# A fused attention and two-MoE kernel on one core: another cost model for spreading attention units, and six places of PSUM for the first MoE once attention is over

## The chip, the cores and the metric

The kernel runs on one core of one Trainium2 chip. The metric is the device time of one execution in microseconds. Before the change the median of three runs is 749.09 us (747.17 to 750.77).

## What is computed

Attention over 4 batches, 8 heads, 576 tokens and 64 channels per head, with a mask by blocks of 64 tokens; its result, as x of 576 x 512 per batch, goes through a first MoE block and that through a second:

```
scores = scale * q @ k.T, masked by blocks of 64;  attn = softmax(scores);  x = attn @ v
xk = mu_k*x + (1-mu_k)*x_prev;  xr = mu_r*x + (1-mu_r)*x_prev        # x_prev: x shifted by a token
k = relu(xk @ w_k);  v = (k*k) @ w_v;  r = sigmoid(xr @ w_r);  x = r*v    # first MoE, 512 -> 1024 -> 512
h = gelu(x @ w_in);  u, v = halves of h;  v = layernorm(v)*g_ln
x = x + (u * (w_sg @ v + b_sg)) @ w_out                                # second MoE
```

All products are of full float32 precision: a factor is split into a high and a low float32r part, and three products stand for one.

## The kernel before

**Attention** is cut into 64 units, one for each batch, head and kind. A unit of kind LO holds tokens 0 to 319, one of kind HI tokens 320 to 575. Their order (L245) is batches 0 and 1 LO (units 0 to 15), batches 0 and 1 HI (16 to 31), then the same for batches 2 and 3 (32 to 63). A unit has three steps: `emit_S` (scores into the PSUM tiles SA and SB, maxima on VectorE, exponentials on ScalarE, normalisation of P on VectorE), `emit_T` (P is turned over through PSUM tile T on TensorE; ScalarE copies out the high part PH, VectorE the low part PL) and `emit_PV` (the product with V into PSUM tile O; ScalarE copies one half out as otmp, VectorE adds the other into xT). Scores run two units ahead of the other steps (`LAG`, L434). The first 16 units (`DIRECT`) use whole float32 products, which the planner's model prices twice as high as split ones.

**The first MoE** (`moe1`, L508) runs over eight halves of 288 tokens (L496), each with 8 tiles of wk, 4 of wr and 4 of wv. A tile is accumulated in PSUM over 12 products of 128x288 (24 for wv). Before a half, `mix` (L475) makes its xh and xl from xT in four chunks of two heads each, so a half needs the attention units of its batch. ScalarE empties a wk tile with a Relu into R (two buffers); the square, the copy kh and the low part kl follow on ScalarE and GpSimd.

**The order of work.** The program is written as a stream of small steps. `Order` holds a model of time in TensorE nanoseconds (`cost`, L112): `pe` moves it on, `at` puts an evacuation into it. While `moe1` runs, the loop at L666 asks at every tick how much of attention should have been issued by now. It emits pieces while `spent_a - base < target(x)` (L671), where x counts halves and `spent_a` is the model time of attention so far. `target` (L652) runs in straight lines between knots: at x = i - 0.15 the units that half i needs must be there (`need`, `MIX_AT`). Its height is `cum(n)`, a sum of `UNIT_NS`, 2000 ns for a LO unit and 3120 for a HI one. What is still missing when the knot is reached is emitted at once (L674). The tile framework then orders each engine's queue by a schedule of its own, so places are read below from the built order.

**PSUM** before the second MoE has eight banks: M with two buffers, T with two, O and SA with one each, and SB, two banks wide. `mtile1` (L148) gives the first MoE its tiles, always from M. When attention is over, T, O, SA and SB stand empty until the second MoE opens its own pool (L703).

**The tail.** With the last unit emitted (L677) the loads of w_in start, and each tick splits two pieces of w_in (`w_split`, L212): per piece Abs on ScalarE (L218), four passes over 128x512 on VectorE (L219, L220, L222, L224), a copy `w` on ScalarE (L227) and a last pass on VectorE (L229). Then x of batch 0 comes back from DRAM and is split into XHL (L661, L693). The second MoE begins with tiles V (`stage_v`, L746).

Of the kernel before, what the change touches and what calls it, by code (L numbers as in the profile page):

```python
# [17 lines left out]
B, H, S = 4, 8, 576  # L18
# [2 lines left out]
CH0 = [0, 64, 192, 320, 448]  # L21
CHN = [64, 128, 128, 128, 128]
CHE = [64, 192, 320, 448, 576]

F64_MIN = struct.unpack("f", struct.pack("I", 896 << 20))[0]
F64_MAX = struct.unpack("f", struct.pack("I", (1151 << 20) - 1))[0]
# [15 lines left out]
class Order:  # L42
# [12 lines left out]
    def pe(self, ns):  # L55
        self.run(self.t)
        self.t += ns
# [43 lines left out]


DIRECT = 16
XT_BUFS = 8
MIX_AT = 0.85
G = 2
X0_AT = 0.55
CONV2 = 2
UNIT_NS = [2000, 3120]


def cost(n):  # L112
    return n / 2.4 + 13
# [3 lines left out]
def fused_kernel(ctx: ExitStack, tc: tile.TileContext, first, qkv_lo, qkv_hi, mu,  # L117
# [21 lines left out]
    def ptile(tag, cols, bufs):  # L139
# [5 lines left out]
        r.append(key)  # L145
        return ps([128, cols], F32, tag, bufs), key

    def mtile1():  # L148
        t, key = ptile("M", 512, 2)
        return t[:, 0:HF], key  # L150

    def mm(out, lhsT, rhs, start=False, stop=False):
# [130 lines left out]
    def split_v(n):  # L283
# [8 lines left out]
        copy(nc.scalar, V[:, 0:nj, odd, :], v)  # L292
        sub(nc.gpsimd, V[:, 0:nj, 1 - odd, :], v, V[:, 0:nj, odd, :].bitcast(F32))

    def emit_S(n):
        b, h, kind = units[n]
        order.need(("sp", n))
        Q, K, KL = splits.pop(n)
        chunks = CHUNKS[kind]
        if n < H and n % 2 and kind == LO:  # L300
            (sa, ka), (sb, kb) = ptile("M", 512, 2), ptile("M", 512, 2)
        else:
            (sa, ka), (sb, kb) = ptile("SA", 512, 1), ptile("SB", 1024, 1)
        stc = {0: sa[:, 0:64], 1: sa[:, 64:256], 2: sb[:, 0:320], 3: sa[:, 0:448]}
        if kind == HI:
            stc[4] = sb[:, 224:800]
        skc = [ka, ka, kb, ka, kb]
        P = probs[n] = pbuf[n % 2]
        pieces = {c: [(0, 288), (288, 576)] if c == 4 else [(0, CHE[c])] for c in chunks}
        pe(sum((2 if n >= DIRECT else 4) * cost(e - a) for c in chunks for a, e in pieces[c])  # L310
           + cost(64) * (n >= DIRECT) * sum(c > 0 for c in chunks))
        mx, sm = smax[n % 4], ssum[n % 4]
        t0, t1 = TOKENS[kind]
        nb = atile([128, 5], F32, "nb", 4)
        rr = atile([128, 5], F32, "rr", 4)
        for c in chunks:
            q0, m, e, st = CH0[c] - TOKENS[kind][0], CHN[c], CHE[c], stc[c]
            for k0, k1 in pieces[c]:
                o = st[0:m, k0:k1]
                if n < DIRECT:  # L320
                    mm(o, Q[:, q0:q0 + m], K[:, k0:k1], start=True, stop=True)
                    continue
                mm(o, Q[:, q0:q0 + m], K[:, k0:k1], start=True)
                if c > 0 and k1 == e:
                    mm(st[:, e - 64:e], mask_l, mask_r)
                mm(o, Q[:, q0:q0 + m], KL[:, k0:k1], stop=True)

        def red(cs):
            for c in cs:
                m, e, st = CHN[c], CHE[c], stc[c]  # L330
                nc.vector.tensor_reduce(out=mx[0:m, c:c + 1], in_=st[0:m, 0:e], axis=AX.X, op=ALU.max)
            s = slice(cs[0], cs[-1] + 1)
            nc.scalar.activation(out=nb[:, s], in_=mx[:, s], func=AF.Copy, scale=-0.125)

        def exp(cs):
            for c in cs:
                m, e, st, po = CHN[c], CHE[c], stc[c], POFF[c]
                nc.scalar.activation(out=P[0:m, po:po + e], in_=st[0:m, 0:e], func=AF.Exp,  # L338
                                     scale=0.125, bias=nb[0:m, c:c + 1], accum_out=sm[0:m, c, 0:1])

        def norm():
            cs = slice(chunks[0], chunks[-1] + 1)
            nc.vector.tensor_reduce(out=rr[:, cs], in_=sm[:, cs], axis=AX.X, op=ALU.add)
            nc.vector.reciprocal(out=rr[:, cs], in_=rr[:, cs])
            for c in chunks:
                m, e, o = CHN[c], CHE[c], POFF[c]

                nc.vector.tensor_scalar(out=P[0:m, o:o + e], in0=P[0:m, o:o + e],  # L348
                                        scalar1=rr[0:m, c:c + 1], scalar2=None, op0=ALU.mult, op1=ALU.add,
                                        accum_out=junk[0:m, c:c + 1])  # L350

        parts = [[0, 1, 2]] if kind == LO else [[3], [4]]
        t = 0
        for cs in parts:
            w = sum(CHE[c] for c in cs)
            sk = [skc[c] for c in cs]
            at(t, lambda cs=cs: red(cs), *sk)
            t += 1.1 * w
            at(t + 100, lambda cs=cs: exp(cs), *sk, ("P", n))
        at(t + 1.2 * w + 500, norm, ("P", n))  # L360
# [32 lines left out]
    def emit_PV(n):  # L393
        b, h, kind = units[n]
        order.need(("sv", n))
        V = vs.pop(n)
        odd = h % 2
        ot, ok = ptile("O", 512, 1)
        order.need(("PT", n))
        prods = PRODS[kind]  # L400
        pe(sum((2 if n >= DIRECT else 4) * cost(p[4]) for p in prods))
        t0, t1 = TOKENS[kind]
        for x, (j, u, src, q0, nq) in enumerate(prods):
            for i, part in enumerate(trans[n, u]):
                v = V[:, 64 * j:64 * j + 128] if n < DIRECT else V[:, j].rearrange("p a d -> p (a d)")
                mm(ot[:, q0 - t0:q0 - t0 + nq], v,
                   part[:, src:src + nq], start=x == 0 and i == 0, stop=x == len(prods) - 1 and i == len(trans[n, u]) - 1)
        for u in range(len(GROUPS[kind])):
            trans.pop((n, u))
        if (b, h // 2) not in xt:  # L410
            t = xt[b, h // 2] = mtile([128, S + 2], F32, "xT", XT_BUFS)
            nc.gpsimd.memset(t[:, 0:1], 0.0)
        t = xt[b, h // 2]
        r0, r1 = 64 * odd, 64 - 64 * odd
        tmp = atile([128, 320], F32, "otmp", 1)
        w = t1 - t0

        def ev1():
            copy(nc.scalar, tmp[r0:r0 + 64, 0:w], ot[r1:r1 + 64, 0:w])

        def ev2():
            nc.vector.tensor_tensor(out=t[r0:r0 + 64, 1 + t0:1 + t1], in0=ot[r0:r0 + 64, 0:w],  # L422
                                    in1=tmp[r0:r0 + 64, 0:w], op=ALU.add)

        def ev():
            copy(nc.scalar, t[r0:r0 + 64, 1 + t0:1 + t1], ot[0:64, 0:w])

        if n < DIRECT:
            at(0, ev, ok, ("x", b, kind))
            return  # L430
        at(0, ev1, ok)
        at(600, ev2, ok, ("x", b, kind))
# [208 lines left out]
    for i in range(1, len(halves)):  # L641
        if need[i] > knots[-1][1]:
            knots.append((i - 1 + MIX_AT, need[i]))
    unit_t = [UNIT_NS[kind] for b, h, kind in units]
    base = spent_a

    def cum(n):
        return sum(unit_t[H:n])

    all_t = cum(NU)  # L650

    def target(x):  # L652
# [13 lines left out]
    for x in moe1():  # L666
# [10 lines left out]
        if done >= NU and phase2 is None:  # L677
# [2 lines left out]
            order.need(*[k for k in list(order.due) if k[0] in ("x", "ps", "PT", "P")])  # L680
            acm.__exit__(None, None, None)
            phase2 = True
            wcm, wtile = pool("moe2w", side="right")

            def wt2(shape, dt):
# [283 lines left out]
```

## Time and profile before

| what | value |
|---|---|
| median of three runs | 749.09 us |
| time of the profiled execution | 752.42 us |
| its span, first to last instruction | 750.5 us |
| mean granted TensorE clock | 0.973 of full speed |
| PE busy | 699.5 us (93%), 4824 matmuls |
| DVE / ACT / POOL busy | 529.5 / 434.8 / 329.4 us |

The profiled execution is 3.3 us longer than the median. Matmuls overlap in the pipeline, so a group's mean duration (some 300 ns) is not what one costs in a stream: that is read from a stretch of time and the number of matmuls in it. A wait is given in brackets in the rows, with what ended it.

### The profile page before, as it was taken

The numbers are of one execution on the slowest core, as the hardware profiler recorded it, in microseconds if no ns is written. First come the engines' busy times: TensorE is split into PE (matmuls) and PEld (weight loads), VectorE is DVE, ScalarE is ACT, GpSimd is POOL, SyncE is SP. The second block draws the span as 40 slices with busy tenths as digits, with TensorE's granted clock in tenths as the row PEclk, the third lists the DMA queues.
The fourth block names the chain that finished last, engine by engine and source line by source line (L and its number), as shares of the span: only waits on it lengthen the run. The fifth ranks groups of instructions, "written<-read, shape, count | busy, mean of one in ns | idle before, by whom it ended". The sixth has DMA issues, their size and how long they took to land.

```text
span 750.5 us, 13615 instructions
## 1 busy us (share of the span) xinstructions
PE 699.5 (93%) x4824; PEld 660.2 (88%) x4824; DVE 529.5 (71%) x1306; ACT 434.8 (58%) x1247; POOL 329.4 (44%) x381
## 2 busy tenths in 40 slices
PE   7878989998799899999899989988999999999998
PEld 5567869998799799999799979977999999999997
DVE  5999987778885766674885988479698736636323
ACT  4878768866795697794795788355361212122020
POOL 1437657834583386483584466134034204103021
PEclk9998999999999999999999999989999999999999
DMA  8571124223212222223222220062460120120101
GB/s 264 216 257 34 33 92 147 64 87 104 83 59 69 78 69 77 58 83 103 79 90 80 79 94 4 25 232 64 142 251 2 38 89 1 41 87 1 56 9 64
DMA packets 30724, 65.78 MB, mean 88 GB/s; under 512 B 5280, under 2 KB 16544, under 8 KB 30656
## 3 DMA queue, kind: packets, MB, share of 16 engines
q1 hardware_dynamic: 30512, 64.91, 26.5%
q8 instruction: 38, 0.62, 0.4%
q14 instruction: 30, 0.25, 0.1%
q10 hardware_dynamic: 144, 0.00, 0.0%
HBM read 55.47 MB, written 9.44 MB: 86 GB/s over the span
## 4 chain that ended last, share of the span: by engine, by line
PE 68%; DVE 14%; ACT 11%; DMA 3%; issue 3%; POOL 1%; SPq 0%; ACTq 0%; POOLq 0%; DVEq 0%
PE M L153 39%; PE O L153 14%; PE V L153 5%; PE T L370 5%; PE SB L153 3%; PE SA L153 3%; ACT P L338 2%; DVE u L222 2%; ACT PH L157 2%; DVE u L224 1%; DVE u L219 1%; DVE P L348 1%; DVE t L484 1%; DVE u L220 1%; DMA w<-w_k_dram 1%
## 5 line engine op out<-in xcount | busy, mean ns | idle before, releaser
L153 PE MATMUL M<-xh,w 128*128 128x288 f32 x768 | 178.8, 310 | 12.4 <-ACT xh L157 6.3
L153 PEld LDWEIGHTS M<-xh,w 128*128 128x128 f32 x768 | 133.0, 195 | 16.8 <-ACT R L535 7.9
L153 PE MATMUL M<-xl,w 128*128 128x288 f32 x384 | 117.2, 306 | 1.2 <-DVE xl L168 1.2
L153 PE MATMUL M<-kh,w 128*128 128x288 f32 x512 | 111.9, 300 | 3.7 <-ACT w L227 3.7
L168 DVE TENSOR_TENSOR PL<-T,PH 128x256 fp32r<-128x256 f32 (+3 forms) x128 | 68.9, 542 | 30.5 <-ACT PH L157 29.6
L153 PEld LDWEIGHTS M<-kh,w 128*128 128x128 f32 x512 | 84.7, 189 | 4.1 <-ACT w L227 4.1
L370 PE MATMUL T<-ident,P 128*128 128x128 f32 x480 | 83.5, 286 | 4.2 <-DVE P L348 2.4
L157 ACT ACTIVATE PH<-T 128x384 fp32r<-128x384 f32 (+4 forms) x144 | 68.0, 478 | 30.0 <-PE T L370 27.5
L168 POOL TENSOR_TENSOR KL<-qkv,K 128x576 fp32r<-128x576 f32 (+1 forms) x48 | 60.6, 1263 | 54.3 <-ACT K L157 40.8
L348 DVE TENSOR_SCALAR_CACHE_REDUCE P<-P,rr 64x64 f32<-64x64 f32 (+3 forms) x160 | 79.7, 536 | 1.1
L153 PEld LDWEIGHTS M<-xl,w 128*128 128x128 f32 x384 | 75.3, 196 | 2.2 <-DVE xl L168 1.8
L153 PE MATMUL M<-kl,w 128*128 128x288 f32 x256 | 76.0, 297 | 0.0
L847 POOL TENSOR_TENSOR gt<-gt,U 128x288 f32<-128x288 f32 x32 | 29.3, 920 | 100.5 <-DVE gt L843 100.4
L370 PEld LDWEIGHTS T<-ident,P 128*128 128x128 f32 x480 | 59.7, 147 | 9.1 <-issue 3.0
L168 POOL TENSOR_TENSOR xl<-t,xh 128x288 fp32r<-128x288 f32 x48 | 41.0, 855 | 49.3 <-ACT xh L157 46.8
L168 POOL TENSOR_TENSOR kl<-R,kh 128x288 fp32r<-128x288 f32 x64 | 57.8, 915 | 10.2 <-ACT kh L157 9.6
L168 POOL TENSOR_TENSOR w<-u,w 128x512 fp32r<-128x512 f32 x24 | 35.5, 1482 | 59.4 <-ACT w L227 59.4
L153 PE MATMUL O<-PH,V 128*128 128x256 f32 (+2 forms) x208 | 58.8, 294 | 3.0 <-DVE xT L422 3.0
L168 POOL TENSOR_TENSOR V<-qkv,V 128x320 fp32r<-128x320 f32 (+1 forms) x48 | 39.4, 820 | 45.2 <-ACT V L157 30.4
L153 PE MATMUL O<-PL,V 128*128 128x256 f32 (+2 forms) x208 | 56.3, 289 | 1.6 <-DVE PL L168 1.6
L153 PE MATMUL O<-gh,w 128*128 128x288 f32 x256 | 53.3, 294 | 0.0
L153 PE MATMUL M<-XHL,w 128*128 128x288 f32 x384 | 53.1, 295 | 0.0
(155 smaller groups left out, 1845.1 us busy)
## 6 DMA issues: line engine op xcount, KB each, us to landing
qkv<-qkv_hi_dram SPq DMA_DIRECT2D x32, 576.0 KB, 3.8
qkv<-qkv_lo_dram SPq DMA_DIRECT2D x16, 416.0 KB, 3.3
x2d<-x SPq DMA_DIRECT2D x32, 144.0 KB, 2.0
X<-x2d SPq DMA_DIRECT2D x4, 1152.0 KB
outT_dram<-o SPq DMA_DIRECT2D x32, 144.0 KB, 1.8
w<-w_k_dram SPq DMA_DIRECT2D x8, 512.0 KB
w<-w_v_dram SPq DMA_DIRECT2D x8, 512.0 KB, 7.6
w<-w_in_dram SPq DMA_DIRECT2D x8, 512.0 KB, 8.9
```

The lines of the kernel that those rows point to most:

```text
L153: nc.tensor.matmul(out=out, lhsT=lhsT, rhs=rhs, start=start, stop=stop)
L157: nc.scalar.activation(out=out, in_=in_, func=AF.Copy)
L168: eng.tensor_tensor(out=out, in0=a, in1=b, op=ALU.subtract)
L219: nc.vector.tensor_scalar(out=v, in0=v, scalar1=F64_MIN, scalar2=F64_MAX, op0=ALU.max, op1=ALU.min)
L220: nc.vector.tensor_scalar(out=u, in0=u, scalar1=3, scalar2=0x3FFFFFFF, op0=ALU.logical_shift_left, op1=ALU.bitwise_and)
L222: nc.vector.scalar_tensor_tensor(out=u, in0=high, scalar=-0x40000000, in1=u, op0=ALU.bitwise_and, op1=ALU.bitwise_or)
L224: nc.vector.scalar_tensor_tensor(out=u, in0=low, scalar=29, in1=u, op0=ALU.logical_shift_right, op1=ALU.bitwise_or)
L338: nc.scalar.activation(out=P[0:m, po:po + e], in_=st[0:m, 0:e], func=AF.Exp, scale=0.125, bias=nb[0:m, c:c + 1], accum_out=sm[0:m, c, 0:1])
L348: nc.vector.tensor_scalar(out=P[0:m, o:o + e], in0=P[0:m, o:o + e], scalar1=rr[0:m, c:c + 1], scalar2=None, op0=ALU.mult, op1=ALU.add, acc ...
L370: nc.tensor.transpose(t[:, o:o + 128], P[:, POFF[c] + CH0[j]:POFF[c] + CH0[j] + 128], ident)
L484: nc.vector.scalar_tensor_tensor(out=t1, in0=x[:, s0 + 1:s0 + 1 + HF], scalar=mu_t[:, i, c:c + 1], in1=t1, op0=ALU.mult, op1=ALU.add)
L847: nc.gpsimd.tensor_tensor(out=gt, in0=gt, in1=U[b][:, m, fs], op=ALU.mult)
```

## The change

Two things. First, `UNIT_NS` goes. `cum(n)` is now the sum of the very prices that `emit_S`, `emit_T` and `emit_PV` report to the model (`score_ns`, `out_ns`), with the scores taken two units ahead, as they are emitted. By these formulas a LO unit of the DIRECT kind costs 3098 ns, a HI unit 3080 and a later LO unit 1955. Second, once `att_over` is filled, `mtile1` takes its tiles in turn from T, O, SA, T, M, M. T has two buffers, O and SA one and M two, which makes six places.

```
-UNIT_NS = [2000, 3120]
+PS_BUFS = dict(M=2, T=2, O=1, SA=1)
...
+    att_over = []
     def mtile1():
-        t, key = ptile("M", 512, 2)
+        if att_over:
+            tag = att_over[0]
+            att_over.append(att_over.pop(0))
+        else:
+            tag = "M"
+        t, key = ptile(tag, 512, PS_BUFS[tag])
         return t[:, 0:HF], key
...
+    def score_ns(n):
+        f, cs = (2, CHUNKS[units[n][2]]) if n >= DIRECT else (4, CHUNKS[LO])
+        return sum(f * cost(e - a) for c in cs for a, e in PIECES[c]) + cost(64) * (f == 2) * sum(c > 0 for c in cs)
+
+    def out_ns(n, trans=True):
+        kind = units[n][2]
+        return (sum((2 if n >= DIRECT else 4) * cost(p[4]) for p in PRODS[kind])
+                + trans * sum(len(g) * cost(230) for g, _ in GROUPS[kind]))
...
-    unit_t = [UNIT_NS[kind] for b, h, kind in units]
-    base = spent_a
-
     def cum(n):
-        return sum(unit_t[H:n])
-
+
+        return sum(score_ns(u) for u in range(H, min(NU, n + LAG))) + sum(out_ns(u) for u in range(H, n))
+
+    base = spent_a - cum(H)
...
             phase2 = True
+            att_over += ["T", "O", "SA", "T", "M", "M"]
```

The rest of the diff moves the same formulas out of `emit_S` and `emit_PV`; no product, copy or transfer is added or removed.

**Place 1: TensorE at the start of half 6** (batch 2, tokens 288 to 575). M tiles with xh or xl are products of the half that begins, those with `w_328` its fourth chunk, which waits for the last heads. SA, SB, O and T are attention's. Before:

```order
L153 MATMUL SB_6213<-K_5902,Q_5901 128x288
L153 MATMUL SB_6213<-mask_r_64,mask_l_63 128x64
L153 MATMUL SB_6213<-KL_5903,Q_5901 128x288
L153 MATMUL O_6131<-PL2_6085,V_5748 128x128
L153 MATMUL O_6131<-PH2_6084,V_5748 128x256
L153 MATMUL O_6131<-PL2_6085,V_5748 128x256
L370 MATMUL T_6179<-ident_60,P1_90 128x128 x4
L370 MATMUL T_6195<-ident_60,P1_90 128x128 x3
L153 MATMUL M_5979<-xh_5909,w_328 128x288
L153 MATMUL M_5995<-xh_5909,w_328 128x288
```

and now, a piece of the same stretch:

```order
L162 MATMUL M_6067<-xh_5913,w_219 128x288
L162 MATMUL M_6067<-xh_5913,w_276 128x288
L162 MATMUL M_6067<-xl_5914,w_276 128x288
L162 MATMUL M_6067<-xh_5913,w_276 128x288
L162 MATMUL SA_6101<-K_5906,Q_5905 128x448
L162 MATMUL SA_6101<-mask_r_64,mask_l_63 128x64
L162 MATMUL SA_6101<-KL_5907,Q_5905 128x448
L162 MATMUL O_6013<-PL1_5964,V_5698 128x256
L162 MATMUL O_6013<-PH1_5963,V_5698 128x256
L162 MATMUL O_6013<-PL1_5964,V_5698 128x256
L386 MATMUL T_6048<-ident_60,P1_90 128x128 x2
```

Between the last O product that the half needs and the first product of its fourth chunk stood 34 attention matmuls and none of MoE; now 36 of attention and 19 of MoE. Counted in the same way the half that begins at 2 has none of MoE and 34 of attention before, none and 31 now; half 3: none and 23, now 20 and 23; half 4: 45 and 6, now 33 and 19; half 5: none and 29, now 30 and 34. From the first to the last product of a half's first tile stand 108, 65, 9, 58, 81 and 26 attention matmuls (halves 2 to 7) before, and 54, 12, 8, 19, 27 and 13 now.

**Place 2: TensorE after attention's last product.** Tiles with kh and kl are wv products of half 6, xh_6751 and xl_6752 belong to half 7. Before (O_6734 is the last unit):

```order
L153 MATMUL O_6734<-PH2_6732,V_6600 128x256
L153 MATMUL O_6734<-PL2_6733,V_6600 128x256
L153 MATMUL M_6890<-xh_6751,w_328 128x288
L153 MATMUL M_6924<-xh_6751,w_328 128x288
L153 MATMUL M_6890<-xl_6752,w_328 128x288
```

and now some rows of the stretch that lies between attention's end and the fourth chunk (`w_328`):

```order
L162 MATMUL T_6814<-kh_6011,w_1133 128x288
L162 MATMUL T_6968<-xh_6751,w_164 128x288
L162 MATMUL T_6968<-xl_6752,w_164 128x288
...
L162 MATMUL O_6890<-xh_6751,w_276 128x288
L162 MATMUL O_6890<-xh_6751,w_328 128x288
L162 MATMUL SA_6924<-xh_6751,w_328 128x288
```

Before, the fourth chunk followed at once; now 36 products stand between. From there to the first wr product with the fourth chunk of xl_6940 are 98 products before and 128 now, and from that one to the first V product 124 before and 66 now.

**Place 3: VectorE in the tail.** u and w are the splitting of w_in, XHL that of x for the second MoE, xl_6940 with t1_6963 the fourth chunk's low part for wr of half 7. Before:

```order
L229 SCALAR_TENSOR_TENSOR w_6843<-u_6837,w_6843 128x512
L222 SCALAR_TENSOR_TENSOR u_6863<-w_6775,u_6863 128x512
L168 TENSOR_TENSOR xl_6940<-t1_6963,xh_6939 128x288
L159 CAST XHL_7126<-xl_7131 128x4x288
L224 SCALAR_TENSOR_TENSOR u_6863<-w_6775,u_6863 128x512
```

and now:

```order
L168 CAST XHL_7126<-xl_7131 128x4x288
L228 TENSOR_SCALAR u_6863<-u_6863 128x512
L177 TENSOR_TENSOR XHL_7126<-xl_7131,XHL_7126 128x4x288
L238 SCALAR_TENSOR_TENSOR w_6843<-u_6837,w_6843 128x512
L168 CAST XHL_7126<-xh_7127 128x4x288
L229 TENSOR_SCALAR u_6863<-u_6863 128x512
L177 TENSOR_TENSOR xl_6940<-t1_6963,xh_6939 128x288
```

Three XHL passes have moved ahead of xl_6940 and one pass of u_6863 (L222, now L231) behind it; the rows ahead of these are the same passes in nearly the same order.

## Rows read from the trace of the kernel before

**Rows 1.** The page: busy time, share and count of TensorE, and the granted clock in 40 slices of the span.

```profile
PE 699.5 (93%) x4824; PEld 660.2 (88%) x4824; DVE 529.5 (71%) x1306; ACT 434.8 (58%) x1247; POOL 329.4 (44%) x381
PEclk9998999999999999999999999989999999999999
```

**Rows 2.** Stretches of the span: from and to, length, then busy time and number of instructions for PE, PEld, DVE, ACT and POOL, granted clock, DMA share and GB/s.

```profile
155.00:175.00 20.00, 20.00 (x158) 19.90 (x157) 16.14 (x41) 12.01 (x35) 7.79 (x8) 1.00 0.28 95
175.00:203.00 28.00, 20.77 (x135) 19.32 (x134) 23.41 (x54) 20.73 (x61) 14.03 (x15) 0.88 0.28 86
203.00:249.00 46.00, 45.79 (x358) 45.23 (x357) 33.78 (x82) 34.60 (x105) 27.78 (x36) 1.00 0.19 61
249.00:264.00 15.00, 11.53 (x81) 10.11 (x79) 10.45 (x41) 11.20 (x39) 5.76 (x8) 0.94 0.33 96
361.00:379.00 18.00, 13.79 (x88) 12.52 (x88) 16.08 (x39) 14.96 (x43) 9.43 (x10) 0.91 0.30 100
380.00:396.00 16.00, 15.81 (x125) 15.50 (x124) 13.15 (x29) 14.56 (x45) 13.42 (x16) 1.00 0.24 75
424.00:442.00 18.00, 13.93 (x94) 12.57 (x94) 17.11 (x38) 14.22 (x41) 9.54 (x10) 0.93 0.23 69
488.00:524.00 36.00, 28.59 (x171) 26.09 (x170) 30.96 (x43) 21.97 (x51) 14.75 (x16) 0.86 0.47 154
```

**Rows 3.** The same view of the instructions on tile M alone (here the first MoE's): length, PE, PEld, then DVE and ACT where they touch M.

```profile
155.00:175.00 20.00, 13.44 (x83) 11.33 (x81) 1.79 (x4) 0.00 (x0) 1.00 0.28 95
175.00:203.00 28.00, 4.41 (x22) 3.78 (x23) 0.00 (x0) 0.82 (x2) 0.88 0.28 86
203.00:249.00 46.00, 32.46 (x220) 29.62 (x219) 1.80 (x4) 3.96 (x10) 1.00 0.19 61
249.00:264.00 15.00, 3.57 (x19) 2.83 (x19) 0.00 (x0) 0.82 (x2) 0.94 0.33 96
361.00:379.00 18.00, 3.78 (x22) 3.18 (x22) 0.00 (x0) 0.72 (x2) 0.91 0.30 100
424.00:442.00 18.00, 3.52 (x18) 2.50 (x17) 0.00 (x0) 0.72 (x2) 0.93 0.23 69
488.00:524.00 36.00, 26.04 (x149) 23.74 (x150) 0.00 (x0) 4.67 (x12) 0.86 0.47 154
523.00:535.00 12.00, 12.00 (x92) 12.00 (x92) 1.36 (x3) 0.18 (x1) 1.00 0.11 38
```

**Rows 4.** What TensorE waited for, longest in total first: the first row of 175 to 203 us, then the first two of 488 to 524 us (us in total, times, longest).

```profile
PE SA L153 <- ACT P L338: 5.6, 3, 2.4
...
PE M L153 <- ACT R L535: 4.0, 4, 2.5
PE M L153 <- ACT xh L157: 2.6, 1, 2.6
```

**Rows 5.** TensorE in order of time (start, duration, idle before it and what ended it): the start of half 2, and of half 4.

```profile
187.81 0.28 PE L153 MATMUL O<-PL,V 128*128 128x256 f32 x1
190.46 0.47 PE L153 MATMUL SA<-K,Q 128*128 128x448 f32 x1 [1.60 <-ACT P L338]
195.41 0.53 PE L153 MATMUL M<-xh,w 128*128 128x288 f32 x2 [1.22 <-ACT xh L157]
197.50 0.71 PE L153 MATMUL SA<-K,Q 128*128 128x448 f32 x1 [1.56 <-ACT P L338]
...
303.54 0.28 PE L153 MATMUL O<-PL,V 128*128 128x128 f32 x1
310.24 0.38 PE L153 MATMUL M<-xh,w 128*128 128x288 f32 x1
```

**Rows 6.** The tail in order of time: TensorE from the last attention product to the first V tile.

```profile
492.38 0.28 PE L153 MATMUL O<-PL,V 128*128 128x256 f32 x1
495.25 0.85 PE L153 MATMUL M<-xh,w 128*128 128x288 f32 x2 [2.58 <-ACT xh L157]
513.58 0.40 PE L153 MATMUL M<-xh,w 128*128 128x288 f32 x1 [2.46 <-ACT R L535]
518.23 0.40 PE L153 MATMUL M<-xl,w 128*128 128x288 f32 x1 [0.26 <-DVE xl L168]
535.36 2.91 PE L153 MATMUL V<-w,XHL 128*128 128x512 f32 x12
```

**Rows 7.** ScalarE in the same stretch: the copy that its queue stood behind.

```profile
511.51 0.63 ACT L227 ACTIVATE w<-u 128x512 fp32r<-128x512 f32 x1 [2.30 <-DVE u L224]
```

**Rows 8.** VectorE from the last xl of wk to that of wr and beyond.

```profile
495.23 0.46 DVE L168 TENSOR_TENSOR xl<-t,xh 128x288 fp32r<-128x288 f32 x1 [0.51 <-ACT xh L157]
498.25 1.17 DVE L222 SCALAR_TENSOR_TENSOR u<-w,u 128x512 int32<-128x512 int32 x1
517.13 0.68 DVE L222 SCALAR_TENSOR_TENSOR u<-w,u 128x512 int32<-128x512 int32 x1
517.73 0.45 DVE L168 TENSOR_TENSOR xl<-t,xh 128x288 fp32r<-128x288 f32 x1
518.10 0.75 DVE L159 CAST XHL<-xl 128x1152 fp32r<-128x1152 f32 x1
520.31 1.34 DVE L168 TENSOR_TENSOR XHL<-xl,XHL 128x1152 fp32r<-128x1152 f32 x1
521.58 0.74 DVE L159 CAST XHL<-xh 128x1152 fp32r<-128x1152 f32 x1
```

More of the change, by code (lines that the diff above doesn't have):

```diff
@@ L23 @@
 CHE = [64, 192, 320, 448, 576]
+PIECES = [[(0, 288), (288, 576)] if e == 576 else [(0, e)] for e in CHE]
 F64_MIN = struct.unpack("f", struct.pack("I", 896 << 20))[0]
@@ L308, in emit_S @@
         P = probs[n] = pbuf[n % 2]
-        pieces = {c: [(0, 288), (288, 576)] if c == 4 else [(0, CHE[c])] for c in chunks}
-        pe(sum((2 if n >= DIRECT else 4) * cost(e - a) for c in chunks for a, e in pieces[c])
-           + cost(64) * (n >= DIRECT) * sum(c > 0 for c in chunks))
+        pe(score_ns(n))
         mx, sm = smax[n % 4], ssum[n % 4]
@@ L317, in emit_S @@
             q0, m, e, st = CH0[c] - TOKENS[kind][0], CHN[c], CHE[c], stc[c]
-            for k0, k1 in pieces[c]:
+            for k0, k1 in PIECES[c]:
                 o = st[0:m, k0:k1]
@@ L400, in emit_PV @@
         prods = PRODS[kind]
-        pe(sum((2 if n >= DIRECT else 4) * cost(p[4]) for p in prods))
+        pe(out_ns(n, False))
         t0, t1 = TOKENS[kind]
```

## The prediction

> **What bounds the kernel now.** I read the page first: TensorE is busy for 699.5 of 750.5 us, and the granted clock dips in some slices [rows 1]. So what is to be won lies in the stretches where TensorE waits or runs slowly, and the question is where these are. Next I cut the span into stretches [rows 2] and counted the first MoE's matmuls in each [rows 3]. The reader is to see two kinds. In 203 to 249 us TensorE is busy for 45.8 of 46 us at full clock. In 175 to 203, 249 to 264, 361 to 379 and 424 to 442 us it issues far fewer matmuls per microsecond, only about 20 of each stretch's matmuls are MoE's, and the clock is 0.88 to 0.94. A fifth stretch, 488 to 524 us, is the tail after attention: nearly all MoE, clock 0.86. The waits [rows 4] name the causes. In a bunch, TensorE waits for the exponentials that free SA; in the tail, for R, the emptying of M, and for xh. Last I read the order of time at the places where a half begins [rows 5], and the tail engine by engine [rows 6 to 8].
>
> **Prices.** From 523 to 535 us only MoE's products run, 92 in 12.0 us: 0.130 us each [rows 3]. From 203 to 249 us 220 MoE products take 28.6 us of the 46, so the other 138 cost 17.4/138 = 0.126 us each [rows 2, 3]; I use 0.125. What a stretch loses is its length less its matmuls at these prices; this holds waits and slow clock together.
>
> | stretch | MoE, attention | work | lost |
> |---|---|---|---|
> | A 175 to 203 | 22, 113 | 17.0 | 11.0 us |
> | B 249 to 264 | 19, 62 | 10.2 | 4.8 us |
> | C 361 to 379 | 22, 66 | 11.1 | 6.9 us |
> | D 424 to 442 | 18, 76 | 11.8 | 6.2 us |
> | E 488 to 524 | 149, 22 | 22.1 | 13.9 us |
>
> A to D lose 28.9 us, E 13.9 us. In the rest of the span the change moves little: the first 100 us have nearly the same order, and stages of the second MoE have none of its edits.
>
> **Why the bunches are there.** By the change's formulas the eight DIRECT units 8 to 15 add 24.6 us of model time (the scores run two units ahead, so two of the score steps are HI ones); the old table allowed them 16.0 us. Attention is thus 8.6 us of model time late at the first knot, and since the later entries of the table are nearly right it stays 7 to 8 us late at the knots of halves 2 to 6. Each time this remainder, two or three units, is issued at once. That is a bunch, and it agrees with where A to D lie.
>
> **Part 1, the new cum.** It removes the lag, so units come at an even pace. The built order shows it: attention inside the first tile of halves 2, 3, 5 and 6 falls from 108, 65, 58 and 81 matmuls to 54, 12, 19 and 27. What is left of each loss depends on the cover between the last O product a half needs and its fourth chunk. In A that took from 187.8 to 195.4 us, 7.6 us, with waits; at half 4 from 303.5 to 310.2 us, 6.7 us, with 45 MoE products between and no wait [rows 5]. So the chain through otmp, xT and mix needs 6.4 us or less when TensorE has other work, and up to 7.6 us in a bunch. The new covers are: half 2, 31 attention products, 3.9 us; half 3, 20 MoE and 23 attention, 5.5 us; half 5, 30 and 34, 8.2 us; half 6, 19 and 36, 7.0 us.
> - A: 3.0 us of the chain stay open, and of the 5.6 us of waits on SA [rows 4] half, since half the bunch is left: 2.5 to 3 us. I leave 5.5 of 11.0.
> - B: 1 to 2 us open. I leave 1.5 of 4.8.
> - C and D: covered. I leave 1.0 each, for the waits on P.
>
> Left 9.0 of 28.9, so 20 us gained. The bounds: all of it gone, 27 us (A keeps 2); or no more than A's half and B, 9 us, if the waits move rather than go.
>
> **What pays for it.** The units that stood in bunches now lie in stretches that were full. A HI half is 240 MoE products and 8 units of 27: 31.2 + 27.0 = 58.2 us, or 3.7 attention products per us against 3.0 in 203 to 249 us. The trace has shorter stretches at that density: 155 to 175 us has 75 in 20 us, TensorE busy throughout, DVE 81%; and from 380 to 396 us TensorE is 99% busy with ACT at 91% [rows 2, 3]. So the pace holds for 16 to 20 us; whether for 58 us no row shows. The bounds are nothing, and 6% of some 230 us of HI halves, 14 us, about where ACT's 91% would be past its room. I take 4 us, nearest the two rows that hold.
>
> **Part 2, six places, and the tail.** Before, TensorE stands from 492.7 to 495.3 us for the fourth chunk's xh, and then four times for a Relu [rows 4, 6]. The Relu was late because ScalarE's queue stood 2.30 us behind a `w` copy that waits for VectorE's L224 [rows 7]; TensorE resumes at 513.58 after 2.46 us. With six places TensorE need not stand there. The first wait has 36 products, 4.7 us, in front of it now, so it goes. But VectorE hardly idles in the tail, 31.0 of 36 us [rows 2], and the last wr products wait on its xl, which ends at 518.2 us [rows 6, 8]: that is what is late next. From the xl of wk (495.2) to that xl is 23.0 us of VectorE. The order now puts three XHL passes ahead (0.75 + 1.34 + 0.74 = 2.8 us) and one L222 pass of 0.68 us behind: 25.1 us. TensorE has only 128 products, 16.6 us, to do meanwhile, so it waits some 8 us in all, in other places than before. After the xl 66 products are left, 8.6 us: V begins 33.7 us after 495.2, against 40.2 us now. That is 6.5 us earlier, and 8 products (1.0 us) that lay ahead of attention's end now lie behind it. I take 7 us. V needs its first four pieces of w_in and XHL, both at most a few passes after this xl in the new order, so nothing later holds it. The bounds: 13 us, if VectorE's passes ran at their short prices (L222 took 1.17 and 0.68 us on the same shape [rows 8]) and TensorE set the pace; and nothing or a loss of 2 us, if the Relus stay bound to ScalarE's queue, where `w` copies still stand between them.
>
> **Sum.** 20 + 7 - 4 = 23 us. The profiled execution took 752.4 us, 3.3 us above the median; 752.4 - 23 = 729.4, and against the median 749.1 - 23 = 726 us. A gain of that size is 3%.
>
> **Rivals.**
> 1. *The lag moves and is not removed* (chance 0.13). TensorE's queue is fixed at build time; wherever a unit's exponentials come later than the schedule thought, the queue stands and the MoE products behind it stand too. For it: half 2 still begins behind 54 attention products without MoE between. Against it: three of four covers have grown past 5 us. Gain 9 from the bunches and 4 from the tail, less 6: 742 us.
> 2. *The even pace is too fast for the softmax chain: slower* (0.07). Within bunch A a unit follows the last after 7.0 us, SA from 190.46 to 197.50 [rows 5], with nearly all engines on attention alone. An even HI half gives a unit 7.3 us, and MoE's evacuations share ScalarE and VectorE with it. If the cycle of SA, exponentials and P grows past 7.3 us, TensorE pays the excess for each of 32 HI units. It decides from 8.1 us on, where 32 x 0.8 = 26 us eat the gain; at 8.5 us the kernel takes 749 - 27 + 38 = 760 us. Against it: 155 to 175 us holds the pace.
> 3. *Six places slow the clock in the tail* (0.05). In E the granted clock is 0.86 already, after waits of 2.5 us [rows 2, 6]. Waits split over six tiles could leave it at the lower of its two levels, 1.2 GHz, all through: the 128 products ahead of the xl would take 33 us and set the pace, V would begin at 33 + 8.6 = 42 us after 495.2, 2 us later than now. Then 749 - 20 + 4 + 2 = 735 us. The Trainium skill (TensorE: Matmul & The Clock Gate, "A second HAM failure mode: psum-queue depth-cycling") speaks against part 2 by such a rule: cycling through PSUM banks gave one kernel so many short waits that its clock went up and down. By that rule, as a whole, the tail would gain nothing. The trace neither confirms nor excludes it, as it has only two places.
> 4. *The tail stays where it is, by ScalarE's queue* (0.10): 749 - 20 + 4 = 733 us.
>
> **How the numbers follow.** The forecast, 726 us, gets 0.65; the rivals 0.13, 0.07, 0.05 and 0.10. With the bounds, the best case is 27 + 13 - 2 = 38 us, 711 us, and I cut it at 712; upwards rival 1 at 742 is the last that the range takes in. So 712 to 742 us, which leaves out rival 2 and the outer parts of the others. About 0.5% (3.7 us) is what a measurement of this kernel can tell from no change. Faster by more: the forecast, rivals 3 and 4 and most of rival 1, 0.88. Within: 0.05, from rivals 1 and 2. Slower by more: 0.07.
>
> **What would show it.** In the new profile the stretches at the starts of halves 3, 5 and 6 should issue above 7 matmuls per us at full clock, half 2 should keep one gap of some 5 us, and the waits of SA for ACT's P should fall by half or more. In the tail no wait for R above 1 us on a free place, but waits for xl or R of about 8 us in sum, VectorE over 90% busy until the first wv products, and V some 37 us after attention's last product instead of 43. The mean granted clock should rise above 0.98. The prediction is wrong if SA's waits are as long in sum and only spread out (rival 2), if the clock in the tail is below 0.7 (rival 3), or if V begins over 41 us after attention's end (rival 4).

## The result, and the profile after

The changed kernel takes 717.07 us (median of four runs, 715.23 to 717.90) where the kernel before takes 749.71 us (four runs) on the same chip: a ratio of 0.9566, 95% interval 0.9534 to 0.9598, or 32.6 us less. Measured again later, in five rounds, it took 715.27 us against 748.36, ratio 0.9555 [0.9529, 0.9581]. The forecast was 726 us, its range 712 to 742. The profiled execution shown below took 717.42 us, its span is 715.6 us and its mean granted clock 0.987; it stands against one of 752.42 us before.

The page, in the lines that answer to [rows 1]:

```profile
PE 685.5 (96%) x4824; PEld 650.9 (91%) x4824; DVE 535.7 (75%) x1306; ACT 435.2 (61%) x1247; POOL 327.6 (46%) x381
...
PEclk9998998999999999999999999999999999999999
```

As many matmuls as before, in 35 us less. Of the two dips of the clock in the row before, the one in the tail (slice 27) is gone; that of slice 4 stays, and slice 7, ahead of half 1, has a new one. First the whole stretch from half 1's first product to attention's last one, before and then after. As in [rows 2], the columns are from and to, length, busy time and count of PE, PEld, DVE, ACT and POOL, granted clock, DMA share and GB/s; the second row of each fence is the same stretch for tile M alone, as in [rows 3].

```profile
120.00:492.70 372.70, 350.84 (x2632) 341.98 (x2630) 272.18 (x712) 274.79 (x831) 206.83 (x240) 0.98 0.24 75
120.00:492.70 372.70, 220.21 (x1458) 200.95 (x1457) 11.30 (x25) 29.04 (x72) 0.98 0.24 75
```

```profile
123.00:462.00 339.00, 336.16 (x2615) 332.33 (x2614) 275.25 (x704) 273.56 (x826) 202.19 (x238) 1.00 0.26 80
123.00:462.00 339.00, 227.34 (x1435) 199.48 (x1433) 10.73 (x24) 28.92 (x72) 1.00 0.26 80
```

At the prediction's prices (0.130 and 0.125 us) the work is 1458 x 0.130 + 1174 x 0.125 = 336.3 us before and 1435 x 0.130 + 1180 x 0.125 = 334.1 us after. So 36.4 us of this stretch were lost before and 4.9 us are lost now. Of the whole gain of 34.9 us in span, this is 31.5.

Now the single places after: the start of half 2, the even stretch behind it, the starts of halves 3, 5 and 6, and the tail; then the first five for tile M alone.

```profile
180.00:205.00 25.00, 23.71 (x185) 23.15 (x183) 21.90 (x55) 22.13 (x67) 17.57 (x22) 1.00 0.32 102
205.00:236.00 31.00, 30.55 (x238) 29.77 (x237) 26.15 (x64) 25.95 (x77) 18.67 (x24) 1.00 0.22 67
236.00:250.00 14.00, 14.00 (x114) 14.00 (x113) 10.30 (x36) 11.00 (x35) 5.44 (x9) 1.00 0.35 112
338.00:354.00 16.00, 15.97 (x124) 15.66 (x123) 15.58 (x35) 12.37 (x35) 7.55 (x8) 1.00 0.38 124
400.00:416.00 16.00, 15.16 (x118) 14.69 (x117) 13.16 (x33) 12.34 (x37) 8.41 (x9) 1.00 0.33 101
462.00:500.00 38.00, 32.60 (x226) 31.43 (x225) 35.85 (x53) 22.29 (x50) 15.76 (x16) 0.96 0.39 130
...
180.00:205.00 25.00, 11.35 (x77) 10.32 (x76) 0.44 (x1) 2.33 (x6) 1.00 0.32 102
205.00:236.00 31.00, 20.66 (x129) 17.65 (x127) 0.90 (x2) 2.40 (x6) 1.00 0.22 67
236.00:250.00 14.00, 10.38 (x67) 9.16 (x67) 0.89 (x2) 0.82 (x2) 1.00 0.35 112
338.00:354.00 16.00, 11.97 (x72) 9.83 (x70) 0.89 (x2) 0.39 (x1) 1.00 0.38 124
400.00:416.00 16.00, 9.54 (x61) 8.12 (x60) 0.45 (x1) 0.81 (x2) 1.00 0.33 101
```

The bunches are gone: 61 to 77 MoE products stand where 18 to 22 stood, every stretch but the tail is at full clock, and what is lost comes to 1.5 us at half 2 (25.0 less 77 x 0.130 + 108 x 0.125 = 23.5), nothing at half 3, 0.1 at half 5 and 0.9 at half 6. What TensorE waited for from 100 to 462 us, the longest, which lies ahead of half 1, and the one that was first before [rows 4]:

```profile
PE T L386 <- DVE P L364: 2.0, 1, 2.0
...
PE SA L162 <- ACT P L354: 0.7, 2, 0.5
```

At the start of half 2 the order of time, which answers to [rows 5], is: the last O product that the half needs, two short waits, and the first product of the fourth chunk 5.7 us later. That product waits for nothing: in ScalarE's order, the last row here, its xh was done at 188.96 us, 4.5 us after the O product, although it had stood behind the exponentials P.

```profile
184.49 0.28 PE L162 MATMUL O<-PL,V 128*128 128x256 f32 x1
...
186.33 0.38 PE L162 MATMUL O<-PH,V 128*128 128x256 f32 x1 [0.80 <-DVE xT L438]
...
187.44 0.47 PE L162 MATMUL SA<-K,Q 128*128 128x448 f32 x1 [0.50 <-ACT P L354]
...
190.15 0.43 PE L162 MATMUL M<-xh,w 128*128 128x288 f32 x2
...
188.51 0.45 ACT L166 ACTIVATE xh<-t 128x288 fp32r<-128x288 f32 x1
```

**The tail.** TensorE from attention's last product to the first V tile, answering to [rows 6]:

```profile
461.63 0.28 PE L162 MATMUL O<-PL,V 128*128 128x256 f32 x1
...
475.62 0.40 PE L162 MATMUL M<-xh,w 128*128 128x288 f32 x1 [1.48 <-ACT R L551]
477.65 0.40 PE L162 MATMUL T<-xh,w 128*128 128x288 f32 x1 [0.97 <-ACT xh L166]
479.93 0.40 PE L162 MATMUL T<-xl,w 128*128 128x288 f32 x1 [0.51 <-POOL xl L177]
484.59 0.40 PE L162 MATMUL T<-xh,w 128*128 128x288 f32 x1 [2.40 <-ACT xh L166]
...
491.79 0.29 PE L162 MATMUL T<-xl,w 128*128 128x288 f32 x1
...
500.60 0.86 PE L162 MATMUL V<-w,XHL 128*128 128x512 f32 x3
```

V begins 39.0 us after attention's last product, where it took 43.0 (37.5 us in the second profile of the changed kernel). One wait for R of 1.48 us is left, on M; the longest is now for the fourth chunk's xh. Its cause is on VectorE, which answers to [rows 8]:

```profile
481.16 0.68 DVE L238 SCALAR_TENSOR_TENSOR w<-u,w 128x512 fp32r<-128x512 f32 x1
481.76 1.29 DVE L233 SCALAR_TENSOR_TENSOR u<-w,u 128x512 int32<-128x512 int32 x1
482.98 1.08 DVE L500 SCALAR_TENSOR_TENSOR t<-xT,mu_t,t 128x288 f32<-128x288 f32 x1
```

The mix of the fourth chunk (`t`) stands behind two passes on w_in, and ScalarE's xh, which needs t, follows at 484.09. Behind the wait of 2.40 us TensorE's clock falls for some 4 us, to 1.2 GHz, the lower of its two levels, for the most part of them (granted clock 0.60): 21 products take the time of 31 at full speed (4.0 / 0.130), 1.3 us lost:

```profile
485.00:489.00 4.00, 4.00 (x21) 4.00 (x21) 4.00 (x4) 2.04 (x5) 3.13 (x4) 0.60 0.00 0
```

So the gain in the profiled pair divides into 31.5 us of losses and 2.2 of less work between half 1 and attention's end, and 4.0 in the tail, less 3.0 because half 1 began at 122.9 us and not at 119.9. That last part is chance: the same kernel begins half 1 at 121.1 us in its second profile, and the kernel of run 1, with the same order on TensorE until shortly before attention's end, at 120.3.

### The profile page after: what moved, and what is told of

It is laid out like the page before. It is cut to its first block, busy times and chain, and to the rows that moved or that the text cites. A ratio compares the mean times of both kernels' runs of the same rounds, so it can differ in the third digit from the quotient of the medians.

```text
span 715.6 us, 13612 instructions
## 1 busy us (share of the span) xinstructions
PE 685.5 (96%) x4824; PEld 650.9 (91%) x4824; DVE 535.7 (75%) x1306; ACT 435.2 (61%) x1247; POOL 327.6 (46%) x381
## 4 chain that ended last, share of the span: by engine, by line
PE 74%; DVE 14%; DMA 6%; ACT 2%; issue 2%; SPq 0%; POOL 0%; DVEq 0%; ACTq 0%; POOLq 0%
PE M L162 40%; PE O L162 14%; PE T L386 6%; PE V L162 5%; PE SA L162 4%; PE SB L162 4%; DVE u L231 3%; DMA w<-w_v_dram 3%; DMA w<-w_k_dram 2%; DVE u L233 2%; DVE P L364 1%; DVE t L500 1%; DVE u L228 1%; DVE u L229 1%; DVE stats L347 1%
## 5 line engine op out<-in xcount | busy, mean ns | idle before, releaser
L162 PE MATMUL M<-xh,w 128*128 128x288 f32 x704 | 162.4, 305 | 2.4 <-ACT R L551 2.3
L162 PEld LDWEIGHTS M<-xh,w 128*128 128x128 f32 x704 | 119.5, 191 | 4.5 <-ACT R L551 3.5
L162 PE MATMUL M<-xl,w 128*128 128x288 f32 x352 | 105.3, 300 | 0.3 <-POOL xl L177 0.3
L162 PE MATMUL M<-kh,w 128*128 128x288 f32 x448 | 104.4, 304 | 1.2 <-POOL w L177 1.0
L386 PE MATMUL T<-ident,P 128*128 128x128 f32 x480 | 82.0, 282 | 5.6 <-DVE P L364 5.5
L162 PEld LDWEIGHTS M<-kh,w 128*128 128x128 f32 x448 | 75.6, 189 | 1.9 <-POOL w L177 1.5
L162 PEld LDWEIGHTS M<-xl,w 128*128 128x128 f32 x352 | 67.3, 191 | 0.8 <-POOL xl L177 0.6
L162 PE MATMUL M<-kl,w 128*128 128x288 f32 x224 | 67.2, 300 | 0.0
L162 PE MATMUL O<-PH,V 128*128 128x256 f32 (+2 forms) x208 | 57.2, 284 | 0.9 <-DVE xT L438 0.8
L832 ACT ACTIVATE U<-M 128x288 f32<-128x288 f32 x32 | 13.1, 409 | 67.2 <-PE M L162 67.2
```

The source lines that it names most:

```text
L162: nc.tensor.matmul(out=out, lhsT=lhsT, rhs=rhs, start=start, stop=stop)
L386: nc.tensor.transpose(t[:, o:o + 128], P[:, POFF[c] + CH0[j]:POFF[c] + CH0[j] + 128], ident)
L832: nc.scalar.activation(out=U[b][:, m, fs], in_=p, func=AF.Gelu_apprx_tanh)
```

## Experiments

The theory that I held on seeing this: the wrong price of eight DIRECT units is the cause, the lag it makes is most of the time, and in the tail the splitting of w_in sets the end. Each kernel is the changed one with the edit shown.

**1. The new cum alone; M keeps two places.**

```
-            att_over += ["T", "O", "SA", "T", "M", "M"]
```

> The new cum alone; M keeps its two places after attention. Theory (the bunches, which part 1 removes, gave 31 of the 35 us between the two traces, the tail 4): 718 to 723 us, and V begins some 43 us after attention's last product, as before. Rival (the six places give more than the tail shows, or the two need each other): 728 us or more.

718.66 us against 749.55, ratio 0.9586 [0.9558, 0.9614]. Run again in five rounds, beside the changed kernel:

> The new cum alone once more, five rounds beside the changed kernel on the same chip, to size the places. Theory (the tail's 5 us between the two traces are real): 719 to 721 us and 3 to 5 us above the changed kernel. Rival (about 2 us are left in the end, as the medians so far said): 1 to 2.5 us above it.

> The changed kernel once more, as the other side of that comparison: 715 to 718 us.

717.76 us, 0.959 [0.9565, 0.9615], and the changed kernel 715.27 us, 0.9555 [0.9529, 0.9581]. Part 1 is nearly all of the gain; part 2 is worth 1.6 and 2.5 us, not 7. So of the two expectations on the repeat the rival's 1 to 2.5 us held, and the 5 us that the two traces differ by in the tail do not reach the time in full (run 5 shows a part of the reason). In the trace of the first, from attention's end (459.3 us) to V (503.4) TensorE waits for:

```profile
PE M L162 <- ACT R L551: 6.2, 4, 3.5
PE M L162 <- ACT xh L166: 1.4, 1, 1.4
```

The six places do what the prediction said of them, R's waits fall from 6.2 to 1.5 us; but 3.9 us for xh and xl come up behind them.

**2. The six places alone; the old table sets the pace.**

```
-        return sum(score_ns(u) for u in range(H, min(NU, n + LAG))) + sum(out_ns(u) for u in range(H, n))
+        return sum([2000, 3120][units[u][2]] for u in range(H, n))
```

> The old table of unit times with the six places. Theory: the bunches stay (108, 65, 58 and 81 attention matmuls inside the first tiles of halves 2, 3, 5 and 6), only the tail gains 3 to 7 us: 743 to 747 us. Rival (places matter more, since they also free the start of half 7): below 740 us. Rival (the clock in the tail falls with six places): 749 us or more.

746.90 us against 749.55, ratio 0.9962 [0.994, 0.9985]: 2.7 us. The bunches stay, with 8.2 us of waits of SA for P in the trace. The tail gains a little less than the 3 to 7 us expected. The two parts hardly depend on each other.

**3. The old table with one price put right, M on two places.**

```
-        return sum(score_ns(u) for u in range(H, min(NU, n + LAG))) + sum(out_ns(u) for u in range(H, n))
+        return sum(3098 if u < DIRECT else [2000, 3120][units[u][2]] for u in range(H, n))
...
-            att_over += ["T", "O", "SA", "T", "M", "M"]
```

> The old table, two places, but 3098 ns for the units 8 to 15 in place of 2000, nothing else. Theory (the one wrong price made a lag that stays to the end): as the new cum alone, 717 to 723 us. Rival (the other half of the new model, scores counted two units ahead, does it): at least half of the loss stays, 733 us or more.

715.45 us against 749.55, ratio 0.9539 [0.9513, 0.9566]: 34.1 us less. This one number, 3098 for 2000, carries the whole of part 1; the rest of the exact model is not needed, and the kernel comes out 1.5 us below the expectation's range and 3.2 us below run 1, which has the exact model on two places. Why, the runs do not show.

**4. The lag put back.** The changed kernel, with attention held 8.5 us of model time behind the target between knots.

```
-        while done < NU and spent_a - base < target(x) and 4 * units[done][0] + units[done][1] // 2 < free_x:
+        while done < NU and spent_a - base + 8500.0 < target(x) and 4 * units[done][0] + units[done][1] // 2 < free_x:
```

> The changed kernel with a lag of 8.5 us put back: attention is issued only when the model stands 8.5 us behind its target, slopes, prices and places as changed. Theory (lag makes bunches, bunches make the loss): 742 to 748 us, with waits of SA for the exponentials again. Rival (the gain is in the slopes of the model, not in the lag): 725 us or less.

740.04 us against 749.55, ratio 0.9867 [0.9833, 0.99]: 23 us of the gain are gone. The time lies 2 us below the 742 to 748 expected and far from the rival's 725. The trace shows the bunches back at halves 2, 3, 5 and 6, whole and then tile M alone:

```profile
177.00:205.00 28.00, 24.39 (x175) 21.96 (x174) 26.47 (x67) 25.03 (x74) 17.71 (x21) 1.00 0.31 105
244.00:260.00 16.00, 13.71 (x90) 12.33 (x90) 11.50 (x42) 13.51 (x45) 8.82 (x12) 0.89 0.17 55
349.00:367.00 18.00, 14.33 (x96) 13.16 (x95) 16.23 (x39) 14.29 (x41) 9.45 (x9) 0.92 0.25 82
412.00:432.00 20.00, 16.48 (x112) 15.32 (x110) 17.79 (x40) 15.12 (x44) 10.31 (x10) 0.91 0.32 97
...
177.00:205.00 28.00, 8.14 (x55) 7.29 (x54) 0.00 (x0) 1.57 (x4) 1.00 0.31 105
244.00:260.00 16.00, 5.80 (x33) 5.18 (x34) 0.00 (x0) 0.82 (x2) 0.89 0.17 55
349.00:367.00 18.00, 5.27 (x27) 4.26 (x27) 0.45 (x1) 0.00 (x0) 0.92 0.25 82
412.00:432.00 20.00, 4.50 (x28) 3.66 (x26) 0.44 (x1) 0.00 (x0) 0.91 0.32 97
```

By the same prices they lose 5.8, 4.6, 5.9 and 5.9 us, 22.2 in all, where the four places of the changed kernel lose 2.5: 19.7 us more. The two profiled executions differ by 20.6 us (737.98 and 717.42), so these stretches account for nearly all that the edit costs. So the lag as such, made in another way, brings the loss.

**5. Table of 3 with six places.**

```
-        return sum(score_ns(u) for u in range(H, min(NU, n + LAG))) + sum(out_ns(u) for u in range(H, n))
+        return sum(3098 if u < DIRECT else [2000, 3120][units[u][2]] for u in range(H, n))
```

> The old table with 3098 ns for units 8 to 15, with the six places. Theory (the places give 1.6 to 2.7 us whatever the pace, as the two single runs showed): 713 to 714 us. Rival (in that order the tail is covered already and the places give nothing): 715 to 716 us.

713.30 us against 749.82, ratio 0.9513 [0.9487, 0.9539]. It beats both kernels, the changed one by 2 to 4 us. It also shows where some of part 2's gain goes: attention's end to V is 38.5 us here and 43.5 in run 3, 5.0 less, but the time after V is 216.3 against 214.8 us. ScalarE, and then TensorE, after V:

```profile
515.43 0.63 ACT L236 ACTIVATE w<-u 128x512 fp32r<-128x512 f32 x1 [2.19 <-DVE u L233]
515.97 0.40 ACT L832 ACTIVATE U<-M 128x288 f32<-128x288 f32 x1
518.14 0.63 ACT L236 ACTIVATE w<-u 128x512 fp32r<-128x512 f32 x1 [1.77 <-DVE u L233]
518.68 0.39 ACT L832 ACTIVATE U<-M 128x288 f32<-128x288 f32 x1
```

```profile
522.84 1.33 PE L162 MATMUL M<-XHL,w 128*128 128x288 f32 x8 [1.87 <-ACT U L832]
```

The same stall as in [rows 7] one stage on: the emptying of M (now U's) stands in ScalarE's queue behind `w` copies that wait for VectorE. The second profile of the changed kernel has this wait too (1.1 us; 37.5 us to V, 216.4 after), and so have runs 2, 4, 6 and 7 (1.0 to 2.0 us; 216.2 to 216.5 after V); of the profiles with six places and the whole splitting of w_in only the first of the changed kernel has not (215.0 after V). The kernel before, run 3 and both profiles of run 1, all with two places, have none (214.7 to 215.1), nor have the three kernels of run 8, which split less of w_in (214.7 to 214.9). So the wait comes with six places and the splitting together and takes some 1.5 us of the 4 to 5 that the tail gains; that it comes because V begins while more of the splitting is still in the queues is likely, but not shown.

**6. Attention 4 us early instead of late.**

```
-        while done < NU and spent_a - base < target(x) and 4 * units[done][0] + units[done][1] // 2 < free_x:
+        while done < NU and spent_a - base < target(x) + 4000.0 and 4 * units[done][0] + units[done][1] // 2 < free_x:
```

> The changed kernel with attention issued 4 us of model time ahead of the target. In the built order the covers of halves 3 to 7 grow to 5.5 us or more, but half 2 begins behind 84 attention matmuls instead of 54. Theory (cover decides, and the chain needs 6 us or so of it): half 2 loses 2 to 4 us, the others 0 to 2 us gained: 716 to 721 us. Rival (the earlier the better): below 715 us.

723.47 us against 749.82, ratio 0.9631 [0.9592, 0.9671]: some 6 us slower than the changed kernel, and above what both expectations gave. One bunch is back, at half 2, with 84 attention products in the half's first tile (54 in the changed kernel); whole, then tile M:

```profile
180.00:200.00 20.00, 15.59 (x103) 14.08 (x102) 18.64 (x44) 16.30 (x48) 10.77 (x12) 0.91 0.27 90
180.00:200.00 20.00, 4.48 (x24) 3.63 (x24) 0.00 (x0) 0.72 (x2) 0.91 0.27 90
```

It loses 20.0 - 24 x 0.130 - 79 x 0.125 = 7.0 us there, against 1.5 in the changed kernel, which is nearly the whole difference. Why a lead makes a bunch at this place and not at the later knots, I did not follow up.

**7. The knots later, at i - 0.05.**

```
-MIX_AT = 0.85
+MIX_AT = 0.95
```

> The changed kernel with MIX_AT 0.95 for 0.85: the same even pace, but the units are due later and mix follows closer. Covers by the built order 3.9, 3.2, 6.1, 6.4 and 5.7 us for halves 2 to 6, and 3.1 us after the last product of attention. Theory (a cover below 6 us leaves the rest open): 2 to 7 us slower than the change, 719 to 724 us. Rival (the pace alone matters, the cover does not): 716 to 718 us.

723.85 us against 749.82, ratio 0.9674 [0.9628, 0.9721], some 7 us slower. The built order has 54, 33, 31, 34 and 48 attention products in the first tiles of halves 2 to 6 and covers of 3.9, 3.2, 6.1, 6.4 and 5.7 us; attention ends at 471.0 us. The changed kernel has 54, 12, 8, 19 and 27: with the knot so close to the half, units reach into its first tile again. From half 1 to attention's end the kernel loses 13.8 us by the prediction's prices, where the changed one loses 4.9, but not where the covers are shortest: the start of half 2 (175 to 200 us) loses 1.6 us and that of half 3 (232 to 256 us) 0.5, and TensorE's longest waits are 2.0 us for an R at 419 us and 1.2 us for an xl at 325 us. So the time came out as the theory of the cover said, but the trace does not bear that theory out, and the cause of the 7 us stays open.

**8. What sets the tail.** Three kernels take work off it. First the four VectorE passes over each piece of w_in (the other three are put under the same condition):

```
-        nc.vector.tensor_scalar(out=v, in0=v, scalar1=F64_MIN, scalar2=F64_MAX, op0=ALU.max, op1=ALU.min)
+        if key[0] != "win":
+            nc.vector.tensor_scalar(out=v, in0=v, scalar1=F64_MIN, scalar2=F64_MAX, op0=ALU.max, op1=ALU.min)
...
```

> The changed kernel without VectorE's first four passes over each piece of w_in (so the second MoE runs on wrong weights); loads, ScalarE's copies and the last pass stay. Theory (the tail after attention is set by VectorE's passes, through ScalarE's queue): V begins 31 to 34 us after attention's last product instead of 39, and the kernel takes 709 to 712 us. Rival (the tail is set by the Relu, square, copy and subtract chain on R's two buffers, or by the clock): 715 to 717 us.

Then all of a piece's split, with GpSimd filling the pair:

```
+        if key[0] == "win":
+            pair = w1[key] = tp([128, 2, 512], F32R)
+            nc.gpsimd.memset(pair.bitcast(F32), 0.01)
+            return
```

> The changed kernel without any splitting of w_in: the loads stay, and GpSimd fills each pair with a constant in one pass, so neither ScalarE nor VectorE works on w_in (the second MoE runs on a constant in place of w_in). Theory (the tail is set by ScalarE's and VectorE's queues together, and taking VectorE's four passes away left ScalarE full): V begins 31 to 34 us after attention's last product instead of 39, 709 to 713 us. Rival (the chain Relu, square, kh, kl on R's two buffers sets the tail by itself): V at 37 us or more, 715 to 717 us.

and last the same with VectorE filling it (`nc.vector.memset`):

> The changed kernel without any splitting of w_in: each piece's pair is filled with a constant by one short VectorE instruction, where the run before (e13_no_win_split) had GpSimd fill it, 8 times 0.94 us between its copies; the second MoE so runs on other weights. Theory (the tail is late because the queues of ScalarE, VectorE and GpSimd, taken together, are shared with the splitting of w_in): with all of it gone TensorE's waits between attention's end and the first V tile fall from 4.1 us there to 1 to 2 us, V begins 31 to 34 us after the last attention product, and the time is 709 to 712 us. Rival (the last half's own chain, fourth chunk to Relu to square to kl to wv, sets the tail whatever else the engines do): waits of 4 us stay, V begins 36 us or more after, and the time is 712 to 715 us, as in that run.

The times are 716.10 us (ratio 0.9549 [0.952, 0.9579]), 712.80 us (0.9523 [0.9497, 0.9549]) and 708.09 us (0.9463 [0.9436, 0.949]). The second MoE runs on other weights in all three. The stretch from attention's end to V, one row each:

```profile
461.00:498.00 37.00, 32.63 (x227) 31.47 (x226) 17.71 (x24) 22.55 (x52) 14.61 (x16) 0.95 0.40 134
```

```profile
459.00:495.00 36.00, 31.78 (x231) 30.58 (x230) 11.66 (x16) 14.94 (x36) 19.60 (x22) 1.00 0.41 138
```

```profile
460.00:492.00 32.00, 31.49 (x237) 31.21 (x236) 18.64 (x25) 15.34 (x36) 14.52 (x16) 1.00 0.45 155
```

Halving VectorE's work alone (35.9 to 17.7 us) brings nothing clear: V begins 37.9 us after attention's end, against 39.0 and 37.5 in the two profiles of the changed kernel, and the time is the rival's 715 to 717 us, not the theory's 709 to 712; ScalarE's `w` copies and VectorE's last passes are still in the queues. In the second kernel the time is the theory's 709 to 713 us, but V begins after 36.4 us, between the theory's 31 to 34 and the rival's 37. GpSimd's fills (six of 0.94 us in this stretch, two of them, 1.83 us, directly in front) hold up its xl:

```profile
PE T L162 <- POOL xl L177: 2.3, 1, 2.3
```

In the third, where eight fills of 0.91 us are all that VectorE does for w_in, the waits of TensorE in this stretch come to 0.5 us, V begins 31.5 us after attention's end, and the time, 1 us below the least that the theory gave, is 7.2 us below the changed kernel's second measurement. The last half's own chain therefore fits under TensorE's work; the splitting of w_in, through the queues of ScalarE and VectorE, is what the tail pays, and taking the larger part of VectorE's share away is not enough.

## Why the prediction was right, and where its sizes were off

**The mechanism of part 1** was right: one price too low, a lag, bunches at four knots, and no bunches once units come at an even pace. Runs 3 and 4 show it from both sides. One thing it leaves open: by the change's formulas attention is 6.8 us late at the knot of half 4 too, yet no bunch stands there. In the kernel before 300 to 340 us hold 193 MoE and 120 other products, 40.1 us of work in 40.0, and in run 4 as well the bunches come at halves 2, 3, 5 and 6 only.

**"Left 9.0 of 28.9"** was too careful. The four places now lose 2.5 us (1.5, 0, 0.1, 0.9). The step that failed is A: I left half of the SA waits and 3.0 us of the chain open because only 3.9 us cover it, and took the chain to need 6.4 us or so. But the chain through otmp, xT and mix took 4.5 us to the end of xh, TensorE did not wait for it at all, and SA waited 0.7 us. I had taken the chain's length from a bunch, where it shares its engines with two or three more units, and from half 4, where the 6.7 us were the length of the cover and not of the chain. ScalarE's row at half 4, in the kernel before, shows the chain's end: 307.74 us, 4.2 us after the O product at 303.54.

```profile
307.29 0.45 ACT L157 ACTIVATE xh<-t 128x288 fp32r<-128x288 f32 x1 [0.62 <-DVE t L484]
```

**What the table of losses left out.** A to D held 28.9 of the 36.4 us that were lost between half 1 and attention's end. The other 7.5 us lie in stretches that I did not count, 2.2 of them from 264 to 300 us with a wait of 1.2 us for R near 283 us, and about half of them come from the counting: a matmul that crosses an edge counts on both sides, so 13 stretches that join from 119.9 to 492.7 us lose 32.9 us in sum and 36.5 as one. The whole stretch now loses 4.9 us.

**"I take 4 us"** for the pay-back was wrong by 4: none is to be seen. From 205 to 236 us TensorE issues 3.5 attention products per us ((238 - 129) / 31) and loses 0.6 us in 31. The two short rows at the new density, which held, were the right ones to go by.

**"I take 7 us"** for the tail was too much. Its median effect is 1.6 to 2.7 us in four pairs (runs 1 and 2, their repeat, and run 3 with run 5). The traces give 4 to 5 us up to V. The six places took the waits for R away, as said; what I named as next, VectorE's xl of wr, was not waited for, since the fourth chunk's mix and xh were late before it, 2.4 us, and the clock fell behind that wait (1.3 us). In all but one of the profiles with six places and the whole splitting 1.0 to 2.0 us more go at U. The bound below, Relus tied to ScalarE's queue behind `w` copies, named the right queues but the wrong instruction in them.

**The sum.** 26.4 us from A to D instead of 20, no pay-back instead of 4, some 5 more from the rest of the stretch, 2 instead of 7 in the tail: about 33 us, where the medians say 32.6. The error of 9 us in the time is three steps too careful and one too bold.

**The rivals.** The lag did not move (1): waits of SA for P are 0.7 us. The pace was not too fast (2): no HI half shows SA waiting over 0.5 us. Six places did not slow the clock through the tail (3): from attention's end to V it is granted 0.96, 0.95, 0.91 and 0.96 with six (the changed kernel twice, runs 2 and 5), and 0.88, 0.88, 0.96 and 0.88 with two (the kernel before, run 1 twice, run 3). The rule of the Trainium skill that I cited there (TensorE: Matmul & The Clock Gate, "A second HAM failure mode: psum-queue depth-cycling") would have cost part 2 its gain; it did not, but something of the kind is in the traces. The dip shown above stands behind a wait of 2.40 us for xh; in the second profile of the changed kernel a dip of the same size (0.62 from 476 to 480 us) stands behind waits of 1.48 and 0.97 us, and in run 5 one of 0.57 (477 to 481 us) behind four of 0.45 to 0.94 us on M and T. Each is the only long dip of its tail, and each is as long as the one shown, which cost 1.3 us. The tail did not stay where it was (4), but by the medians it came nearer to that than to my 7 us.

**What was to be seen.** Halves 3, 5 and 6 issue 8.1, 7.8 and 7.4 matmuls per us at full clock, VectorE is 94% busy in the tail (35.85 of 38 us), and the mean clock is 0.987, as forecast. Half 2's gap of 5 us is not there. In the tail one wait for R is above 1 us (1.48), the waits come to 5.4 us in place of some 8, and V comes after 39.0 us, and 37.5 in the second profile, where I said some 37.

## What to carry to other kernels

When work is spread by a model, add up the model's own charges between two knots and compare them with what the plan allows: one wrong entry makes a lag that no later entry pays back, and it showed as a bunch at four of the five knots behind it here. Read the length of a dependent chain from the end of its own last row, where its engines are free: neither in the bunch that is to be dissolved, nor by the next product on TensorE, which may stand where it does for another reason. More buffers moved part of the wait here (7.6 us of it became 5.4, behind other instructions in the same queues): to see what a stage pays for side work, take that work off all the engines that share it.

## What the runs showed of the hardware that was not expected

The same waits met a different clock in two executions of one program. In the first profile of the changed kernel waits of 1.48, 0.97 and 0.51 us left 462 to 484.5 us at a granted clock of 1.00, and one of 2.40 us was followed by 4 us at 0.60. In the second, waits of 1.48 and 0.97 us were followed by 4 us at 0.62 (476 to 480 us), and a later one of 2.04 us left 482.8 to 497 us at 1.00. So the length of the last wait alone does not tell whether the clock falls behind it.

GpSimd's fill of a pair, 128 x 1024 elements, took 0.94 us; two of these directly ahead of a copy kept TensorE 2.3 us waiting for an xl, in a stretch where VectorE was busy for 11.7 of 36 us.
